# Softmax row sums from columns of ones beside the values, and routing logits gathered by transposes, in a fused attention and expert kernel

## The chip, the cores and the metric

The kernel runs on one core of a Trainium2 chip. The metric is the device time of one execution in microseconds; the median of the runs is compared. The engines are named as in the profile: PE is TensorE's matmuls and PEld its weight loads, DVE is VectorE, ACT is ScalarE, POOL is GpSimd, and SP is SyncE, which issues the loads here.

## The reference

Eight batches of eight heads, 576 positions in nine chunks of 64, 64 numbers to a head. Attention runs inside each chunk, and the result goes to an expert layer in which each of the 4,608 tokens takes one of eight experts.

```python
scores = scale * np.matmul(q_c, k_c.transpose(0, 1, 2, 4, 3))
scores = scores - np.max(scores, axis=-1, keepdims=True)
attn = np.exp(scores)
attn = attn / (np.sum(attn, axis=-1, keepdims=True) + 1e-09)
out = np.matmul(attn, v_c)
...
logits = x @ w_gate                      # x: 4608 x 512, w_gate: 512 x 8
expert_idx = np.argmax(logits, axis=1)
probs = softmax(logits); gate_w = probs[n, expert_idx[n]]
...
h = np.maximum(xe @ w1[e], 0.0)          # 512 -> 1024, for the tokens of expert e
out[mask] = gate_w[mask, None] * (h @ w2[e])
```

## The kernel before

**Two stages.** The attention stage computes the softmax attention, the logits and the routing; its end overlaps with the first slots of the expert stage, which gathers the tokens of an expert by indirect transfers (`xg`), multiplies them with weights that are split into a high and a low part (`whi`, `wlo`), and scatters the result. From about 110 us on the program is the expert stage.

**Groups.** The attention stage runs over 18 groups of two tiles. A tile is 128 rows (two chunks `c` of 64) with all eight heads; a head is `m` (2) times `hp` (4). The loop works on three groups at once. In iteration g, TensorE gets in this order: the scores of group g (64 products of 64x64, line 240, into the pair of banks S), the selection of the logits of group g-3 (`sel_`, line 1009), the transposes of the exponentials of g-1 into banks U and V (`attn_t`, line 288), the transposes of the attention result of g-2 into T and Q (`x_t`, line 322), the value products of g-1 back into U and V (`attn_v`, line 298), and the logits of g-2 into bank L (`logits_p`, line 334). Between `x_t` and `attn_v` every third group has four small matmuls of a routing step in bank K (lines 394 to 399).

**Softmax.** VectorE takes the row maximum `mx` (line 259), subtracts it (line 260), and sums the exponentials of the group before (`soft_c`, line 269). ScalarE computes the exponential (`soft_b`, line 265), adds 1e-9 to the sums (`soft_e`, line 275), and copies the transposes out of U and V (`at`, line 289) and out of T and Q (`xT`, line 324). VectorE then takes the reciprocal of the sums (`soft_d`, line 280) and multiplies: one product a tile, from bank U or V into the output block `xb` (`x_out`, line 312).

**Logits.** `logits_p` multiplies quarters of `xT` with the gate weights in four parts, 32 partitions apart, so that bank L gets 4 partial sums for each of eight experts, at partitions 0, 32, 64 and 96. ScalarE copies this to `lp` (line 1018). `sel_` multiplies `lp` with `sel_g`, a 0/1 matrix that adds the four parts and brings tokens onto partitions, eight columns a tile, into a place of bank L for a batch of 4 or 6 tiles. At a batch's end ScalarE copies the logits to `lg` (the step "c" of `route`, line 358), and `route` hands out its many small operations over the next groups.

**Order.** PE, DVE, ACT and POOL run in the program's order (a manual schedule). SyncE's queue is ordered by a planner, by when each load's buffer is ready. Its loads are 128x512 pieces of keys (`kb`, line 210) and queries (`qt`, line 212), halves of values (`vb`, line 216) and pieces of weights (`raw`, line 1031), 256 KB each. Eight are in flight; each load waits for the one eight places ahead of it. Three buffers `kb`, three `vb` and three `qt` are turned over; `load_qk(g+3)` and `load_v(g+2)` stand at the end of iteration g. A row of values of 64 positions has two groups of partitions, `m::2`, with zeros in the other's place: that is why `vb` is cleared at the start (by VectorE for `vb[0]`, by ScalarE for the other two).

Of the kernel before, what the change touches and what calls it, by code (L numbers as in the profile page):

```python
# [18 lines left out]
P = 128  # L19
NT = 4608  # L20
D = 512
# [25 lines left out]
def attn_moe_kernel(ctx: ExitStack, tc: tile.TileContext, q, k, v, wg, w, out):  # L47
# [76 lines left out]
    vb = [(ep if i == 1 else kv).tile([P, 2, G, 512], F32, name=f"vb{i}") for i in range(NB)]  # L124
# [14 lines left out]
    nc.vector.memset(vb[0], 0.0)  # L139
    for t in vb[1:]:  # L140
        nc.scalar.copy(t.rearrange("p m g x -> p (m g x)"), zero.broadcast_to([P, 2 * G * 512]))
    for _ in range(WARM):
        nc.tensor.matmul(pw, ones, ones.unsqueeze(1).broadcast_to([P, 4, P]), start=True, stop=True)
    for n in (192, 192, 192, BLK, BLK, BLK):
        nc.tensor.matmul(pw.rearrange("p a b -> p (a b)")[:, 0:n], warm[:, 0:P], warm[:, 0:n], start=True, stop=True)
    iota_i = xg[0][0][:, 0:P].bitcast(I32)
# [22 lines left out]
    nc.vector.tensor_scalar(ident, iota_f[:, 0:P], pid[:, 0:1], None, ALU.is_equal)  # L169
    tri = kv.tile([P, P], BF16, name="tri")  # L170
# [4 lines left out]
    sel_g = kv.tile([P, E], F32, name="sel_g")  # L175
    nc.vector.tensor_tensor(sel_g, ident[:, 0:E], ident[:, 32:32 + E], ALU.add)
    nc.vector.tensor_tensor(sel_g, sel_g, ident[:, 64:64 + E], ALU.add)
    nc.vector.tensor_tensor(sel_g, sel_g, ident[:, 96:96 + E], ALU.add)


# [46 lines left out]
    def keep(n):  # L227

        for _ in range(n):
            nc.tensor.matmul(pR.rearrange("p (a b) -> p a b", b=P), ones,  # L230
                             ones.unsqueeze(1).broadcast_to([P, 4, P]), start=True, stop=True)
# [45 lines left out]
    def soft_d(su):  # L277
        suf = su.rearrange("p h o -> p (h o)")
        ri = sm.tile([P, NH, 1], F32, name="ri", bufs=3)
        nc.vector.reciprocal(ri.rearrange("p h o -> p (h o)"), suf)  # L280
        return ri
# [9 lines left out]

    def attn_v(g, at):
        px = [one["U"], one["V"]]
# [7 lines left out]
        return px  # L301
# [3 lines left out]
    def x_out(g, px, ri, xt):  # L305
        r0 = g * G % RB

        t = g * G - XB * RB
        assert t < 0 or t in stored
        r4 = ri.rearrange("p (m i h) o -> p i h m o", i=G, m=2)  # L310
        for i in range(G):
            nc.vector.tensor_tensor(
                xt[:, r0 + i, 0:D].rearrange("p (m h d) -> p h m d", m=2, d=64),
                px[i].rearrange("p (h m d) -> p h m d", m=2, d=64),
                r4[:, i, :, :, :].broadcast_to([P, 4, 2, 64]), ALU.mult)
# [12 lines left out]
    pR = bank("K", [P, 512])  # L328
# [10 lines left out]
    def route(b, pl):  # L339
# [16 lines left out]
        yield "c"  # L356
        lg = small("lg")
        nc.scalar.copy(lg, pl[:, 0:n, :])
# [425 lines left out]
    def scratch(shape):  # L784
# [4 lines left out]
        t = vb[0].rearrange("p m g x -> p (m g x)")[:, used[0]:used[0] + n]  # L789
# [210 lines left out]
    pls = [None]  # L1000

    def sel_(g):
        b = [i for i in range(NBAT) if first[i] <= g * G][-1]
        if g * G == first[b]:
            o = b % 2 * NMAX * E
            pls[0] = pL[:, o:o + BATCHES[b] * E].rearrange("p (a b) -> p a b", b=E)
        lp = st_l.pop(g)
        for i in range(G):
            nc.tensor.matmul(pls[0][:, g * G - first[b] + i, :], lp[:, i * P:(i + 1) * P], sel_g,
                             start=True, stop=True)  # L1010
        if (g + 1) * G == first[b + 1]:
            r = route(b, pls[0])
            active.append([r, next(r), False])
# [32 lines left out]
    for g in range(NG):  # L1046
# [12 lines left out]
        if gl >= 1:  # L1059
            sel_(gl - 1)  # L1060
            advance("c")
        if ga >= 0:
# [3 lines left out]
            su = soft_c(st_e.pop(ga))  # L1066
        if gl >= 0:
            st_x[gl] = x_t(gl, xb[gl * G // RB % XB])
        if g + 1 < NG:
            if ga >= 0:  # L1070
                soft_e(su)
            st_e[g] = soft_a(ps, 1 if g else G)
            soft_b(st_e[g])
        else:
            soft_b(st_e[g])
            soft_e(su)
# [4 lines left out]
            turns["S"] = 0  # L1081
        pauses()
# [6 lines left out]
        if ga >= 0:  # L1089
            px = attn_v(ga, at)  # L1090
# [9 lines left out]
        if ga >= 0:  # L1100
            ri = soft_d(su)
            x_out(ga, px, ri, xb[ga * G // RB % XB])
# [12 lines left out]
    advance("c")  # L1115
    su = soft_c(ex)
# [3 lines left out]
    soft_e(su)  # L1120
    advance("a")
    st_x[g - 1] = x_t(g - 1, xb[(g - 1) * G // RB % XB])
    px = attn_v(g, at)
    advance("t")
    logits(g - 1)
    ri = soft_d(su)
    x_out(g, px, ri, xb[g * G // RB % XB])
# [4 lines left out]
    advance("c")  # L1132
# [12 lines left out]
    advance("c")  # L1145
# [181 lines left out]
```

## Time and profile before

| | before |
|---|---|
| median of 3 runs (lowest to highest) | 566.22 us (565.96 to 566.27) |
| the profiled execution, its span | 564.68 us, 562.9 us |
| PE busy | 550.6 us, 98% of the span |
| PEld busy | 489.4 us, 87% |
| DVE busy | 422.9 us, 75% |
| ACT busy | 278.4 us, 49% |
| POOL busy | 241.2 us, 43% |
| chain that ended last | PE 74%, issue 4%, POOL 1%, DVE 1% |
| granted TensorE clock, mean | 0.997 |

A busy share is an average over the whole program. The two stages have different limits, so the stretch of a stage says more than the table. The chain is followed back from the last instruction, at each step to what released it. In the timelines, rows of one operation that follow each other are put together: the first column is the start, the second the busy time of all of them, and xN is how many. An idle gap before a row stands in brackets, with what ended it. A busy matmul row overlaps the next one a little, so paces are read from starts.

### The profile page before, as it was taken

How to read it: one execution, taken by the hardware profiler on the slowest of the kernel's cores; microseconds unless marked ns; L12 is line 12 of the kernel's file. 1: busy time of each engine (PE TensorE's matmuls, PEld its weight loads, DVE VectorE, ACT ScalarE, POOL GpSimd, SP SyncE). 2: the span in 40 equal slices, each digit the busy share in tenths (PEclk: the TensorE clock that was granted, in tenths of full speed). 3: DMA queues.
4: the chain of work that ended last, by engine and by line, in shares of the span. 5: the costliest groups of instructions: out<-in, count | busy, mean ns of one | idle time of the engine just before them, and what ended most of it. 6: DMA issues, size and time to landing. Idle time of an engine off the chain costs nothing.

```text
span 562.9 us, 13225 instructions
## 1 busy us (share of the span) xinstructions
PE 550.6 (98%) x4735; PEld 489.4 (87%) x4735; DVE 422.9 (75%) x898; ACT 278.4 (49%) x473; POOL 241.2 (43%) x271
## 2 busy tenths in 40 slices
PE   7999999999999999999999999999999999999995
PEld 5788888788898989889998999988999998898993
DVE  7999999977677986988868875667666566766663
ACT  5667767651336553656546553444443444544332
POOL 3125665476533743537433642351515235250422
PEclk9999999999999999999999999999999999999998
DMA  8999999444764722265435633474522356211201
GB/s 299 381 368 358 398 388 398 153 170 160 267 220 142 237 83 54 68 205 171 146 127 151 211 87 114 157 281 132 215 61 81 120 164 210 65 36 29 68 2 58
DMA packets 51173, 99.03 MB, mean 176 GB/s; under 512 B 13696, under 2 KB 27008, under 8 KB 47488
## 3 DMA queue, kind: packets, MB, share of 16 engines
q0 software_dynamic: 18352, 58.30, 29.9%
q1 hardware_dynamic: 32432, 38.83, 20.4%
q8 instruction: 67, 1.10, 0.8%
q10 hardware_dynamic: 288, 0.52, 0.2%
q14 instruction: 34, 0.28, 0.2%
HBM read 106.59 MB, written 20.22 MB: 225 GB/s over the span
## 4 chain that ended last, share of the span: by engine, by line
PE 74%; issue 4%; POOL 1%; DVE 1%; ACT 0%; POOLq 0%; DVEq 0%
PE psS L637 26%; PE psL L637 8%; PE psU L735 5%; PE psU L736 5%; PE psU L737 5%; PE psV L735 5%; PE psV L736 5%; PE psV L737 5%; PE psK L750 2%; PE psK L748 2%; PE psS L641 2%; PE psK L736 1%; PE psK L737 1%; PE psK L735 1%; PE psT L620 1%
## 5 line engine op out<-in xcount | busy, mean ns | idle before, releaser
L77 DVE TENSOR_TENSOR wlo<-raw,whi 128x1024 fp32r<-128x1024 f32 x110 | 134.2, 1220 | 16.2 <-ACT whi L76 15.7
L686 ACT ACTIVATE h<-psS 128x384 fp32r<-128x384 f32 x84 | 41.3, 492 | 166.9 <-issue 122.1
L544 POOL DMA_INDIRECT raw<-in_w,widx x58 | 67.6, 1165 | 122.9 <-DVE wlo L77 57.5
L76 ACT CAST whi<-raw 128x1024 fp32r<-128x1024 f32 x110 | 114.7, 1043 | 0.0
L637 PE MATMUL psS<-xhi,whi 128*128 128x256 f32 (+2 forms) x368 | 113.9, 311 | 0.0
L637 PE MATMUL psS<-xhi,wlo 128*128 128x256 f32 (+2 forms) x368 | 113.1, 309 | 0.0
L637 PE MATMUL psS<-xlo,whi 128*128 128x256 f32 (+2 forms) x312 | 96.4, 309 | 0.0
L763 POOL DMA_INDIRECT out_y<-y,oid x40 | 44.1, 1102 | 105.6 <-ACTq L668 34.2
L645 DVE SCALAR_TENSOR_TENSOR hl<-psS,h 128x256 fp32r<-128x256 f32 x84 | 35.5, 423 | 57.7 <-ACT h L686 57.5
L562 POOL DMA_INDIRECT xg<-xd,idx x49 | 62.2, 1270 | 27.2 <-issue 13.6
L637 PEld LDWEIGHTS psS<-xhi,whi 128*128 128x128 f32 x368 | 69.3, 188 | 4.1 <-ACT xhi L626 0.5
L637 PEld LDWEIGHTS psS<-xhi,wlo 128*128 128x128 f32 x368 | 69.3, 188 | 0.6
L637 PEld LDWEIGHTS psS<-xlo,whi 128*128 128x128 f32 x312 | 58.6, 188 | 2.4
L735 PE MATMUL psU<-whi,h 128*128 128x512 f32 x120 | 48.3, 403 | 0.0
L735 PE MATMUL psV<-whi,h 128*128 128x512 f32 x120 | 47.3, 394 | 0.0
L736 PE MATMUL psU<-wlo,h 128*128 128x512 f32 x120 | 47.3, 394 | 0.0
L736 PE MATMUL psV<-wlo,h 128*128 128x512 f32 x120 | 47.1, 392 | 0.0
L737 PE MATMUL psU<-whi,hl 128*128 128x512 f32 x112 | 43.9, 392 | 0.0
L737 PE MATMUL psV<-whi,hl 128*128 128x512 f32 x112 | 43.9, 392 | 0.0
L441 POOL DMA_INDIRECT xd<-xb,di x32 | 31.7, 990 | 12.6 <-issue 6.9
L637 PE MATMUL psL<-xhi,wlo 128*128 128x320 f32 (+2 forms) x112 | 35.0, 313 | 0.2 <-issue 0.2
L637 PE MATMUL psL<-xlo,whi 128*128 128x320 f32 (+2 forms) x112 | 34.9, 312 | 0.0
(251 smaller groups left out, 1122.2 us busy)
## 6 DMA issues: line engine op xcount, KB each, us to landing
kb<-in_k SPq DMA_DIRECT2D x36, 256.0 KB
vb<-in_v SPq DMA_DIRECT2D x36, 256.0 KB
qt<-in_q SPq DMA_DIRECT2D x34, 256.0 KB
xg<-xg SPq DMA_DIRECT2D x208, 32.0 KB
raw<-in_w SPq DMA_DIRECT2D x16, 256.0 KB
raw<-in_w,widx POOLq DMA_INDIRECT x58, 4.5
xg<-xd,idx POOLq DMA_INDIRECT x49, 3.5
out_y<-y,oid POOLq DMA_INDIRECT x40, 3.2
```

What stands on the lines that cost most here:

```text
L76: nc.scalar.copy(hi, src)
L77: nc.vector.tensor_tensor(lo, src, hi.bitcast(F32), ALU.subtract)
L441: nc.gpsimd.indirect_dma_start(out=xds[t], out_offset=bass.IndirectOffsetOnAxis(ap=di[:, i, :], axis=0), in_=x, in_offset=None, bounds_che ...
L544: nc.gpsimd.indirect_dma_start(out=raw[c][:, :], out_offset=None, in_=w, in_offset=bass.IndirectOffsetOnAxis(ap=widx[:, u, c:c + 1], axis= ...
L562: nc.gpsimd.indirect_dma_start(out=t[:, :], out_offset=None, in_=xd[0:rows, :], in_offset=bass.IndirectOffsetOnAxis(ap=place(u, h), axis=0 ...
L637: nc.tensor.matmul(ph, a, b[:, kc, WIDE - ph.shape[1]:WIDE], start=kc + i == 0, stop=kc + i == 5 and not late)
L645: nc.vector.scalar_tensor_tensor(o, ph, 0.0, hi.bitcast(F32), ALU.max, ALU.subtract)
L686: nc.scalar.activation(hx[:, EXT:EXT + WIDE], ph, AF.Relu)
L735: nc.tensor.matmul(py, hh, wh, start=f == 0, stop=False)
L736: nc.tensor.matmul(py, hh, wl, start=False, stop=False)
L737: nc.tensor.matmul(py, hl, wh, start=False, stop=f == 7)
L763: nc.gpsimd.indirect_dma_start(out=outs[m], out_offset=bass.IndirectOffsetOnAxis(ap=oid[u % 3][:, m:m + 1], axis=0), in_=y, in_offset=None ...
```

## The change

**Row sums.** Each buffer of values is now eight blocks of 130 columns: a column of ones, 64 values of the first tile, 64 of the second, and a column of ones. The ones are written once (`side`, `sums_of`); they are laid out as the zeros are, ones for the partitions of the block's own half. A value product takes 65 columns of a block for each of two halves, the row sum being the outer column: 130 columns instead of 128. Three of a tile's four `hp` go to bank U or V, the fourth to the last 261 columns of bank K (`pK`); the routing's counts stay in the first 251 (`pR`). `soft_c` and `soft_e` are gone. `soft_d` comes directly behind `attn_v`: four ScalarE operations read the sums out of U, K, V and K, with 1e-9 added, and VectorE takes the reciprocal. `x_out` is three products: U, V and K.

**Values in memory.** The host lays values out so that a block of both tiles is together; a load writes columns 1 to 128 of each block, eight runs of 512 bytes a row in place of one of 4 KB. The rows of the gate weights and of the first expert matrix are permuted on the host to match the new order of heads.

**Logits.** `sel_` transposes `lp`, a tile at a time, into columns 0 to 127 and 384 to 511 of bank L; a reduction on VectorE (`sums`) adds the four parts a group, straight into `lg`. The step "c" is gone.

**Start.** Clearing `vb[1]` and `vb[2]` stands behind the warm-up matmuls in the text; clearing `vb[0]` stands behind the identity matrix, from which `side` is made.

```diff
-    vb = [(ep if i == 1 else kv).tile([P, 2, G, 512], F32, name=f"vb{i}") for i in range(NB)]
+    vb = [(ep if i == 1 else kv).tile([P, 2, 8, 130], F32, name=f"vb{i}") for i in range(NB)]
...
-    nc.vector.memset(vb[0], 0.0)
...
+    side = const.tile([P, 2, 1], F32, name="side")
+    nc.vector.tensor_reduce(side.rearrange("p m o -> p (m o)"), ident.rearrange("p (a m) -> p m a", m=2),
+                            AX.X, ALU.add)
+    nc.vector.memset(vb[0], 0.0)
+    def sums_of(t, put):
+        put(t[:, :, :, 0:130:129], side.unsqueeze(3).broadcast_to([P, 2, 8, 2]))
+    sums_of(vb[0], nc.vector.tensor_copy)
+    for t in vb[1:]:
+        sums_of(t, nc.scalar.copy)
...
     def load_v(g):
         for m in range(2):
-            nc.sync.dma_start(vb[g % NB][m::2, m, :, :], v[g, m::2, :, :])
+            nc.sync.dma_start(vb[g % NB][m::2, m, :, 1:129], v[g, m::2, :, :])
...
-    def soft_c(ex):
+    def soft_d():
         su = sm.tile([P, NH, 1], F32, name="su", bufs=2)
-        nc.vector.tensor_reduce(su.rearrange("p (m h) o -> p m (h o)", m=2),
-                                ex.rearrange("p h k m -> p m h k"), AX.X, ALU.add)
-        return su
-    def soft_e(su):
-        suf = su.rearrange("p h o -> p (h o)")
-        nc.scalar.activation(suf, suf, AF.Copy, bias=1e-9)
...
+        for i in range(G):
+            nc.scalar.activation(su[:, 6 * i:6 * i + 6, 0], one["UV"[i]][:, i * 64:i * 64 + 326:65], AF.Copy, bias=1e-9)
+            nc.scalar.activation(su[:, 12 + 2 * i:14 + 2 * i, 0], pK[:, i * 195:i * 195 + 66:65], AF.Copy, bias=1e-9)
+        nc.vector.reciprocal(ri.rearrange("p h o -> p (h o)"), su.rearrange("p h o -> p (h o)"))
...
+                to = one["UV"[i]][:, hp * 130:(hp + 1) * 130] if hp < 3 else pK[:, i * 131:i * 131 + 130]
                 for c in range(2):
-                    po, o = slice(c * 64, (c + 1) * 64), hp * 128 + c * 64
-                    nc.tensor.matmul(px[i][po, hp * 128:(hp + 1) * 128], at[:, i, hp, po],
-                                     vb[g % NB][:, :, i, o:o + 64],
+                    nc.tensor.matmul(to[po, :], at[:, i, hp, po], vb[g % NB][:, :, hp * 2 + c, i * 65:i * 65 + 65],
                                      start=True, stop=True, tile_position=(0, c * 64))
...
     def sel_(g):
         lp = st_l.pop(g)
         for i in range(G):
-            nc.tensor.matmul(pls[0][:, g * G - first[b] + i, :], lp[:, i * P:(i + 1) * P], sel_g,
-                             start=True, stop=True)
+            nc.tensor.transpose(p4[:, 3 * i, :], lp[:, i * P:(i + 1) * P], ident)
+    def sums(g):
...
+        nc.vector.tensor_reduce(lgs[0][:, o:o + G, :],
+                                p4.rearrange("p a (c e) -> p a e c", e=32)[:, 0::3, 0:E, :], AX.X, ALU.add)
```

**The load queue at the start.** SyncE, places 9 to 17 of the program's loads, before; `vb_122`, `vb_123` and `vb_124` are `vb[0]` to `vb[2]`, `kb_119` to `kb_121` are `kb[0]` to `kb[2]`. The waits name the DMA semaphore of the load eight places ahead and the engine that clears the buffer.

```order
L216 DMA vb_122<-in_v 64x1024 [waits DMAHW0_49,DVE_49]
L216 DMA vb_122<-in_v 64x1024 [waits DMAHW1_49]
L174 DMA wg_sb<-in_wg 128x4x8 [waits DMAHW2_49,Pool_49]
L210 DMA kb_121<-in_k 128x512 [waits DMAHW3_49]
L212 DMA qt<-in_q 128x512 [waits DMAHW4_49]
L210 DMA kb_121<-in_k 128x512 [waits DMAHW5_49]
L212 DMA qt<-in_q 128x512 [waits DMAHW6_49]
L216 DMA vb_123<-in_v 64x1024 [waits DMAHW7_49,Activation_49]
L216 DMA vb_123<-in_v 64x1024 [waits DMAHW0_49]
```

The same nine places of SyncE in the changed program:

```order
L214 DMA kb_121<-in_k 128x512 [waits DMAHW0_49]
L216 DMA qt<-in_q 128x512 [waits DMAHW1_49]
L214 DMA kb_121<-in_k 128x512 [waits DMAHW2_49]
L216 DMA qt<-in_q 128x512 [waits DMAHW3_49]
L184 DMA wg_sb<-in_wg 128x4x8 [waits DMAHW4_49,Pool_49]
L220 DMA vb_123<-in_v 64x8x128 [waits DMAHW5_49,Activation_49]
L220 DMA vb_123<-in_v 64x8x128 [waits DMAHW6_49]
L220 DMA vb_122<-in_v 64x8x128 [waits DMAHW7_49,DVE_49]
L220 DMA vb_122<-in_v 64x8x128 [waits DMAHW0_49]
```

The values of group 0 (`vb_122`) moved from the first two of these places to the last two; the keys and queries of group 2 and the values of group 1 moved ahead of them. The rest of this queue keeps its order.

**ScalarE in one group.** ScalarE in the middle of the stage, from the second copy of `x_t` to the cast of a weight piece, before:

```order
L324 COPY xT_643<-psQ 128x4x128 [waits PE_49]
L275 ACTIVATE su<-su 128x16 [waits DVE_49]
L265 ACTIVATE ex<-ex 128x1024 [waits DVE_49]
L1018 COPY lp<-psL 128x256 [waits PE_49]
L85 CAST whi_1_69<-raw_66 128x512 [waits DMAHW0_49]
```

The same piece of ScalarE in the changed program:

```order
L323 COPY xT_653<-psQ 128x4x128 [waits PE_49]
L269 ACTIVATE ex<-ex 128x1024 [waits DVE_49]
L275 ACTIVATE su<-psU 128x6 [waits PE_49]
L276 ACTIVATE su<-psK 128x2 [waits PE_49]
L275 ACTIVATE su<-psV 128x6
L276 ACTIVATE su<-psK 128x2
L1018 COPY lp<-psL 128x256 [waits DVE_49,PE_49]
L85 CAST whi_1_69<-raw_66 128x512 [waits DMAHW0_49]
```

The one operation on the sums stood ahead of the exponential; the four that read them stand behind it and wait for the value products. The copy of the logits also waits for VectorE now.

**VectorE in one group.** VectorE from the row sums of one group to its second product, before:

```order
L269 TENSOR_REDUCE su<-ex 128x16 [waits Activation_49]
L259 TENSOR_REDUCE mx<-psS 128x16 [waits PE_49]
L260 TENSOR_TENSOR ex<-psS,mx 128x2x512 [waits DVE_49]
L280 RECIPROCAL ri<-su 128x16 [waits Activation_49]
L312 TENSOR_TENSOR xb_116<-psU,ri 128x4x2x64 [waits DVE_49,PE_49]
L312 TENSOR_TENSOR xb_116<-psV,ri 128x4x2x64 [waits PE_49]
```

The same piece of VectorE in the changed program:

```order
L263 TENSOR_REDUCE mx<-psS 128x16 [waits PE_49]
L264 TENSOR_TENSOR ex<-psS,mx 128x2x512 [waits DVE_49]
L1009 TENSOR_REDUCE lg<-psL 128x16 [waits PE_49,Activation_49]
L277 RECIPROCAL ri<-su 128x16 [waits Activation_49]
L309 TENSOR_TENSOR xb_116<-psU,ri 128x384 [waits DVE_49,PE_49]
L309 TENSOR_TENSOR xb_116<-psV,ri 128x384 [waits PE_49]
L312 TENSOR_TENSOR xb_116<-psK,ri 128x2x128 [waits PE_49]
```

The row sums left the head of the group; the reduction of the logits came in behind the subtraction, and the two products became three.

## Rows read from the trace of the kernel before

**Rows 1.** Stretches: bounds, length, busy (count) by engine, granted clock, DMA share, GB/s.

```profile
20.00:45.00 25.00, 25.00 (x527) 21.66 (x523) 22.60 (x39) 18.12 (x38) 5.71 (x9) 1.00 1.01 364
```

**Rows 2.** Timeline of TensorE, one group: start, busy, line, operation, tiles, shapes, count.

```profile
27.57 1.16 PE L240 MATMUL psS<-kb,qt 64*64 64x64 f32 x64
28.66 0.61 PE L1009 MATMUL psL<-sel_g,lp 128*128 128x8 f32 x4
29.12 0.63 PE L288 MATMUL psU<-ident,ex 128*128 128x128 f32 x4
29.59 0.60 PE L288 MATMUL psV<-ident,ex 128*128 128x128 f32 x4
...
31.00 1.09 PE L298 MATMUL psU<-vb,at 128*64 128x128 f32 x16
...
32.90 0.64 PE L334 MATMUL psL<-xT,wg_sb 128*32 128x256 f32 x8
33.47 1.16 PE L240 MATMUL psS<-kb,qt 64*64 64x64 f32 x64
```

**Rows 3.** Timeline of VectorE, one group in the middle of the stage.

```profile
65.17 1.21 DVE L269 TENSOR_REDUCE su<-ex 128x16 f32<-128x1024 f32 x1
66.31 1.21 DVE L259 TENSOR_REDUCE mx<-psS 128x16 f32<-128x1024 f32 x1
67.55 1.23 DVE L260 TENSOR_TENSOR ex<-psS,mx 128x1024 f32<-128x1024 f32 x1
68.69 0.24 DVE L280 RECIPROCAL ri<-su 128x16 f32<-128x16 f32 x1
69.07 0.69 DVE L312 TENSOR_TENSOR xg<-psU,ri 128x512 f32<-128x512 f32 x1
```

**Rows 4.** Timeline of TensorE behind the loop, a selection and what follows it.

```profile
114.16 0.51 PE L1009 MATMUL psL<-sel_g,lp 128*128 128x8 f32 x4
114.52 1.19 PE L585 MATMUL psS<-ident,xg 128*128 128x128 f32 x8
```

**Rows 5.** Timeline of TensorE, the last two scores and the waits behind the last.

```profile
99.83 1.16 PE L240 MATMUL psS<-kb,qt 64*64 64x64 f32 x64
...
105.94 1.16 PE L240 MATMUL psS<-kb,qt 64*64 64x64 f32 x64
107.28 0.61 PE L1009 MATMUL psL<-sel_g,lp 128*128 128x8 f32 x4 [0.19 <-ACT lp L1018]
108.45 0.66 PE L288 MATMUL psU<-ident,ex 128*128 128x128 f32 x4 [0.55 <-DVE xb L312]
```

**Rows 6.** Timeline of ScalarE in the group of Rows 3.

```profile
65.12 0.18 ACT L422 ACTIVATE cb<-psK 128x8 f32<-128x8 f32 x1
65.19 0.19 ACT L423 ACTIVATE ce<-psK 128x8 f32<-128x8 f32 x1
...
68.81 1.06 ACT L265 ACTIVATE ex<-ex 128x1024 f32<-128x1024 f32 x1 [0.75 <-DVE ex L260]
69.77 0.35 ACT L1018 COPY lp<-psL 128x256 f32<-128x256 f32 x1
```

**Rows 7.** Timeline of SyncE's queue: start of issue, time of all, line, transfer, count.

```profile
15.57 0.42 SPq L212 DMA_DIRECT2D qt<-in_q  x1
...
93.62 6.86 SPq L216 DMA_DIRECT2D vb<-in_v  x4
```

**Rows 8.** Timeline of TensorE at the start: first value products, group 1's transposes.

```profile
12.90 1.09 PE L298 MATMUL psU<-vb,at 128*64 128x128 f32 x16 [0.24 <-ACT at L289]
...
17.27 0.66 PE L288 MATMUL psU<-ident,ex 128*128 128x128 f32 x4
```

**Rows 9.** DMA queues from 20 to 45 us: packets, MB, share of 16 engines.

```profile
q1 hardware_dynamic: 4335, 9.03, 99.6%
```

**Rows 10.** DMA packets and queues from 510 to 523 us.

```profile
DMA packets 1329, 0.73 MB, mean 56 GB/s; under 512 B 369, under 2 KB 1266, under 8 KB 1328
...
q1 hardware_dynamic: 1121, 0.46, 13.8%
```

More of the change, by code (lines that the diff above doesn't have):

```diff
@@ L169, in attn_moe_kernel @@
     nc.vector.tensor_scalar(ident, iota_f[:, 0:P], pid[:, 0:1], None, ALU.is_equal)
+    side = const.tile([P, 2, 1], F32, name="side")
[5 more added lines that the diff above has]
+    sums_of(vb[0], nc.vector.tensor_copy)
+    for t in vb[1:]:
+        sums_of(t, nc.scalar.copy)
     tri = kv.tile([P, P], BF16, name="tri")
@@ L229, in keep @@
         for _ in range(n):
-            nc.tensor.matmul(pR.rearrange("p (a b) -> p a b", b=P), ones,
+            nc.tensor.matmul(one["K"].rearrange("p (a b) -> p a b", b=P), ones,
                              ones.unsqueeze(1).broadcast_to([P, 4, P]), start=True, stop=True)
@@ L309, in x_out @@
         assert t < 0 or t in stored
[L310 removed]
+        o = xt[:, r0:r0 + G, 0:D].rearrange("p i (h d) -> p i h d", d=64)
         for i in range(G):
             nc.vector.tensor_tensor(
[L313 to L315 removed]
+                o[:, i, 0:6, :], one["UV"[i]][:, 1 - i:391 - i].rearrange("p (h d) -> p h d", d=65)[:, :, 0:64],
+                ri[:, 6 * i:6 * i + 6, :].broadcast_to([P, 6, 64]), ALU.mult)
+        nc.vector.tensor_tensor(
+            o[:, :, 6:8, :], pK[:, 1:261].rearrange("p (i h d) -> p i h d", i=G, d=65)[:, :, :, 0:64],
+            ri[:, 12:NH, :].rearrange("p (i h) o -> p i h o", i=G).broadcast_to([P, G, 2, 64]), ALU.mult)
     def x_t(g, xt):
@@ L327, in attn_moe_kernel @@
     pL = bank("L", [P, 512])
-    pR = bank("K", [P, 512])
+    pR = one["K"][:, 0:512 - 261]
     def logits_p(g, xT):
@@ L999, in attn_moe_kernel @@
     casts = []
-    pls = [None]
+    lgs = [None]
+    p4 = pL.rearrange("p (a t) -> p a t", t=P)
     def sel_(g):
+        lp = st_l.pop(g)
+        for i in range(G):
+            nc.tensor.transpose(p4[:, 3 * i, :], lp[:, i * P:(i + 1) * P], ident)
+    def sums(g):
         b = [i for i in range(NBAT) if first[i] <= g * G][-1]
         if g * G == first[b]:
[L1005 to L1008, printed above, removed]
-            nc.tensor.matmul(pls[0][:, g * G - first[b] + i, :], lp[:, i * P:(i + 1) * P], sel_g,
-                             start=True, stop=True)
+            lgs[0] = sm.tile([P, NMAX, E], F32, name="lg", bufs=2)[:, 0:BATCHES[b], :]
+        o = g * G - first[b]
+        nc.vector.tensor_reduce(lgs[0][:, o:o + G, :],
+                                p4.rearrange("p a (c e) -> p a e c", e=32)[:, 0::3, 0:E, :], AX.X, ALU.add)
         if (g + 1) * G == first[b + 1]:
-            r = route(b, pls[0])
+            r = route(b, lgs[0])
             active.append([r, next(r), False])
@@ L1081, in attn_moe_kernel @@
             turns["S"] = 0
+        if gl >= 1:
+            sums(gl - 1)
         pauses()
@@ L1089, in attn_moe_kernel @@
         if ga >= 0:
-            px = attn_v(ga, at)
+            attn_v(ga, at)
+            ri = soft_d()
         if g + 1 == NG:
@@ L1114, in attn_moe_kernel @@
     sel_(g - 2)
-    advance("c")
-    su = soft_c(ex)
+    sums(g - 2)
     pauses()
@@ L1131, in attn_moe_kernel @@
     sel_(g - 1)
-    advance("c")
+    sums(g - 1)
     advance("a")
@@ L1144, in attn_moe_kernel @@
     sel_(g)
-    advance("c")
+    sums(g)
     advance("a")
```

52 lines of the change are left out of this document (18 added, 34 removed).

## The prediction

> **What bounds the kernel now.** I read the stretches first, to see which resource is full in the attention stage; then TensorE's timeline of one group, for its pace; then the DMA queue's timeline; then VectorE and ScalarE in one group. The later stage I left alone: the edit has no line there, and the chain of waits is nearly all TensorE from there to the end, so I carry a shift of TensorE at 120 us to the end one for one.
>
> [rows 1] shows the attention stage with nearly everything full: TensorE 25.00 of 25 us, VectorE 22.60, the granted clock at 1.00 (the level of 2.4 GHz), and the 16 DMA engines at a share of 1.01. [rows 2] is one group of two tiles on TensorE: scores at 27.57, next scores at 33.47, so 5.90 us with no wait to speak of. VectorE needs less: in [rows 3] one group runs from 65.17 (row sums of the exponentials) over maximum, subtraction, reciprocal and the two products. Row sums to maximum is 1.14 us; the second product follows the first (69.07, 0.69 long) and ends near 70.3, a pace of 5.1 us. So TensorE sets the pace, VectorE follows at 86% of it, and the loads run some groups ahead of both. VectorE is what the edit relieves, and it isn't the bound.
>
> **The change part by part.**
>
> *TensorE, per group.* The two small matmuls against `sel_g` take 28.66 to 29.12, 0.46 us behind the scores [rows 2]; 0.36 in the tail, behind a full-size matmul [rows 4]. Two transposes take their place: four take 0.47 (29.12 to 29.59), so two 0.24, plus 0 to 0.10 for following the scores; I take 0.27. Gain 0.19 in a group, 0.14 in the tail. The value matmuls stream 130 columns for 128: 1.90 us (31.00 to 32.90) times 2/128 is 0.03 more. Net 0.16 less, 5.74 us a group. The new output starts at odd words of bank K; no row shows such a write, and I take no cost, with 0.9 us (half of 1.90) at most for one group as the far end.
>
> *VectorE.* The row sums go (1.14). The products cover the same 1,024 elements in three operations: 2 x 0.69 becomes about 1.45. A reduction of 64 logits comes, about 0.2. VectorE falls to some 4.3 us. That is worth nothing at a place where TensorE is the bound; it counts where TensorE waits for VectorE, at the end of the stage: [rows 5], 105.94 to 108.45 is 2.51 us for scores and selection, with idle gaps of 0.19 and 0.55 before the next transposes. Without waits these are 1.09 + 0.27 = 1.36: a gain of 1.15.
>
> *ScalarE and the new chain.* Four small reads of the sums stand where one small operation stood, but behind the exponential of the next group in ScalarE's queue, and the reciprocal and products wait for them. That makes a loop per group: maximum to subtraction 1.24, to exponential 1.26, to the next ScalarE operation 0.96 [rows 3, 6], three more at 0.07 apart and 0.18 for the last [rows 6], so 0.42 with the hand-over, reciprocal to product 0.38 [rows 3], products about 1.3. Sum 5.56 us, under TensorE's 5.74. The logits' reduction and up to five routing operations hide in VectorE's wait for ScalarE. Behind the waiting reciprocal stand the products, and for those the transposes into banks U and V; these are not needed before scores and selection have run, 1.9 us after the value matmuls end, and the first product ends about 1.4 us after. So this too I cost at nothing.
>
> *The start.* The queue of loads is built in another order: group 2's keys and queries and group 1's values now stand ahead of group 0's values, which were places 9 and 10 and become 16 and 17. Eight loads are in flight, each waiting for the one eight places ahead. The 17th load of before therefore had landed when the 25th was issued, 15.57 [rows 7]. The same nine loads stand at places 9 to 17 in both kernels, so group 0's value matmuls, which ran at 12.90, now wait until 15.6, and until 16.6 with the price of values below (four such loads). From there: value matmuls 1.9, sums, reciprocal and first product 1.4, transposes: 3.3 us later, where they stood at 17.27 [rows 8]. The shift of TensorE is 16.6 + 3.3 - 17.27 = 2.6 us, or 1.6 if values cost no more.
>
> *The loads of values.* Before, a row of 64 partitions got 4 KB in one run. Now each of its eight blocks is 512 bytes, between the columns of ones. The stage's loads move 9.03 MB in 25 us at 99.6% of 16 engines, 0.72 us for 256 KB; the only transfers in 512-byte runs, the 32 KB spreads, move 0.46 MB in 13 us at 13.8%, which is 1.02 us for 256 KB [rows 9, 10]. The difference, 0.30, is the upper end; the lower end is nothing, if the runs are streamed as before. Each 32 KB spread ends with its own completion packets, eight times as many per byte, and 369 of its 1,329 packets are these small ones, so I take 0.25. The Trainium skill (DMA: Bandwidth & Descriptors, Specifications) puts the line rate at 512 bytes and above; by it the loads would cost no more. The spreads' row speaks against that, and no run here shows it for loads from HBM.
>
> Does that reach TensorE? The lead of the loads is read at group 16. Its second half of keys had landed when the load eight places on was issued, 93.62, and its scores started at 99.83: a lead of 6.2 us [rows 5, 7]; the last query piece comes one place later and is needed half a scores stage later, the same 6.2. Fifteen groups of values, 30 loads, stand ahead: 30 x 0.25 = 7.5, so the data come 1.3 us late. TensorE alone would be at 2.6 - 13 x 0.16 = 0.5 late there. So the loads decide from about group 14 on, 1.3 us.
>
> *Sum.* At scores of group 16: +1.3. Group 17: -0.16, +1.1. Waits at the end of the stage: -1.15, so 0.0. Three selections in the tail at -0.14 and two sets of value matmuls: -0.35. Total -0.4 us, on a profiled execution of 564.68 us (span 562.9); the median of the runs is 1.54 above it, so 566.22 - 0.4 = 565.8. Each 0.01 us per load of values moves this by 0.3 while the loads decide: 0.30 gives +1.1. Below 0.22 TensorE decides again, and 0.20 gives -1.4 (start 2.4, thirteen groups -2.1, then -0.16, -1.15 and -0.35).
>
> **The rivals.**
>
> *Values cost no more.* For it: the bytes are the same and the source is one run. Against: [rows 10]. Then the start costs 1.6, fourteen groups give 2.2, the end 1.15, the tail 0.35: 564.1 us.
>
> *The new chain binds (slower).* If ScalarE's four reads don't overlap, each taking the 0.18 of its whole duration and a hand-over of some 0.07, they cost 1.0 in place of 0.42 and the loop is 6.14 us, 0.4 over TensorE's pace. It decides from 0.6 us for the four reads. Against the pace of before that is 0.24 a group, 3.4 in fourteen, on the start's 2.6, less the tail's 0.35, and the wait at the end stays: +5.6, 571.8 us. For it: the loop has 0.2 of room. Against: the two reads of bank K at 65.12 and 65.19 are 0.07 apart [rows 6].
>
> *Dearer loads (slower).* If a 512-byte run from HBM to a place that is one word off costs more than the spreads show, say 0.35 a load, the data are 4.3 late at group 16 and the sum is +2.6: 568.8 us. It decides from 0.31 a load. For it: no row has such a write. Against: it is one descriptor's work all the same.
>
> *The edit doesn't relieve what it is meant to* is no rival of its own: VectorE's relief is real but costs and gains nothing except at the stage's end, which is in the sum.
>
> **How the numbers follow.** Forecast 0.47, values at no cost 0.27, chain 0.10, dearer loads 0.12, anything else 0.04. What a measurement can tell from no change is about 0.2%, 1.13 us. The forecast's own range is 564.8 to 567.3 (0.20 to 0.30 a load), of which 0.08 is faster by more, 0.03 slower by more. Faster: 0.27 + 0.08 + 0.01 = 0.36. Slower: 0.10 + 0.12 + 0.03 + 0.03 = 0.28. Within: 0.36. The range reaches from 563.4, under the second case, to 569.0, over the dear loads; the chain lies outside, with some ends of the others.
>
> **What would show it.** In the changed profile: the first value matmuls near 16.6 us (15.6 if values are no dearer; 12.9 would refute the start); a group of 5.74 us between scores in the middle of the stage (5.90 or more refutes the gain); from group 14 on, scores that wait for loads, at 101.1 for group 16; the gap before the transposes behind the last scores gone; VectorE near 75% in the stage. In the timeline of ScalarE, four reads of the sums within 0.4 us, behind the exponential. I am wrong if the first value matmuls start early, if reads of the sums lie 0.2 apart, or if the DMA share falls below 1 before 90 us.

## The result, and the profile after

The changed kernel is slower: 573.58 us (573.13 to 574.84) against 566.09 us (564.29 to 566.27) for the kernel before on the same chip, a ratio of 1.0143 [1.0117, 1.0169], or 7.5 us. The profiled execution spans 571.7 us, 8.8 more than before. My forecast was 565.8 us, in a range of 563.4 to 569.0.

The loss is there when the attention stage ends. The timeline of TensorE after (start, busy, line, operation, count), from the last scores to the first product of the experts:

```profile
114.46 1.16 PE L244 MATMUL psS<-kb,qt 64*64 64x64 f32 x64
115.55 0.44 PE L1002 MATMUL psL<-ident,lp 128*128 128x128 f32 x2
116.59 0.66 PE L285 MATMUL psU<-ident,ex 128*128 128x128 f32 x4 [0.60 <-DVE xb L309]
...
126.84 0.39 PE L633 MATMUL psS<-xhi,whi 128*128 128x256 f32 x1
```

The last scores start 8.5 us later than in [rows 5] (105.94). From scores to transposes is 2.13 us where it was 2.51, so 0.4 comes back there. The first product of the experts, of which before's row follows, is 7.85 us late, and that shift stays between 7.3 and 8.3 us up to TensorE's last product.

```profile
118.99 0.39 PE L637 MATMUL psS<-xhi,whi 128*128 128x256 f32 x1
```

So the 8.5 us have to be found between the start and 114.46. The view of what TensorE waited for, after, from 17 to 107 us (total, times, longest), names two waits, neither of which is in before:

```profile
PE psU L297 <- DMA vb<-in_v: 4.6, 1, 4.6
PE psK L297 <- DVE dst L408: 4.3, 4, 1.5
```

**The start: +5.6.** TensorE after, from the first value products to the transposes of group 1:

```profile
17.36 1.57 PE L297 MATMUL psU<-vb,at 128*64 128x130 f32 x12 [4.63 <-DMA vb<-in_v]
...
21.03 1.94 PE L244 MATMUL psS<-kb,qt 64*64 64x64 f32 x64
22.90 0.66 PE L285 MATMUL psU<-ident,ex 128*128 128x128 f32 x4
```

The stretches after (length, busy and count by engine, granted clock, DMA share, GB/s) that go with it:

```profile
14.00:17.00 3.00, 0.00 (x0) 0.00 (x0) 0.26 (x1) 1.06 (x1) 0.00 (x0) 0.83 1.17 311
18.00:19.00 1.00, 1.00 (x14) 1.00 (x12) 0.00 (x0) 0.03 (x1) 0.00 (x0) 0.50 1.05 379
...
22.00:23.00 1.00, 1.00 (x41) 0.93 (x34) 1.00 (x3) 0.00 (x0) 0.97 (x1) 0.61 1.05 330
23.00:24.00 1.00, 1.00 (x10) 1.00 (x11) 1.00 (x2) 0.36 (x1) 0.30 (x1) 1.00 0.92 336
```

TensorE waits for the values and nothing runs on it from 14 to 17 us. The granted clock falls to 0.50, the level of 1.2 GHz, and is back at 1.00 at 23 us. The value products take 3.67 us (17.36 to 21.03) where they took 1.90, and the scores 1.87 (21.03 to 22.90) where they take 1.09. Transposes of group 1 stand at 22.90, 5.6 us behind [rows 8].

**Bank K: +5.0.** TensorE after, a group in which routing counts are in bank K:

```profile
47.92 0.89 PE L297 MATMUL psU<-vb,at 128*64 128x130 f32 x12
50.27 0.44 PE L297 MATMUL psK<-vb,at 128*64 128x130 f32 x4 [1.46 <-DVE dst L408]
```

VectorE over the same time:

```profile
48.24 1.23 DVE L264 TENSOR_TENSOR ex<-psS,mx 128x1024 f32<-128x1024 f32 x1
49.38 0.21 DVE L1009 TENSOR_REDUCE lg<-psL 128x16 f32<-128x64 f32 x1
...
50.05 0.17 DVE L408 TENSOR_TENSOR dst<-psK,oh_b 128x48 f32<-128x48 f32 x1
```

The fourth value product of a tile, the one that goes to bank K, waits until VectorE has read the counts of the routing out of that bank. From U's first product to K's is 0.72 us where nothing waits, and 2.35, 1.88, 1.79 and 1.87 in the four groups with this wait: 1.63 + 1.16 + 1.07 + 1.15 = 5.0 us.

**The rest.** Three rows of scores take longer, 1.32, 1.23 and 1.61 us for 1.16, and cost 0.8 together with small delays beside them; the longest has a short stop inside. The pace gains: one group without waits, after:

```profile
27.29 1.16 PE L244 MATMUL psS<-kb,qt 64*64 64x64 f32 x64
28.38 0.44 PE L1002 MATMUL psL<-ident,lp 128*128 128x128 f32 x2
28.66 0.60 PE L285 MATMUL psU<-ident,ex 128*128 128x128 f32 x4
...
32.99 1.16 PE L244 MATMUL psS<-kb,qt 64*64 64x64 f32 x64
```

That is 5.70 us for 5.90 in [rows 2]. From the scores at 27.29 to the last ones are fourteen groups, and they give 2.9; 0.4 of it are small delays of the kernel before in its last two groups (6.39 and 6.11 us from scores to scores, for 6.22 and 5.90 elsewhere). The sum is 5.6 + 5.0 + 0.8 - 2.9 = 8.5 us, the shift at the last scores.

VectorE is relieved as meant, 17.81 us of 25 where [rows 1] has 22.60. The loads are not, in this stretch and in the queue of SyncE's loads:

```profile
20.00:45.00 25.00, 25.00 (x537) 21.38 (x538) 17.81 (x34) 17.40 (x48) 5.22 (x5) 0.94 1.03 337
```

```profile
q1 hardware_dynamic: 7652, 8.34, 101.4%
```

At a full share they move 8.34 MB where [rows 9] has 9.03, in 7,652 packets for 4,335.

### The profile page after: what moved, and what is told of

The parts are those of the page before. It is cut to its first block, busy times and chain, and to the rows that moved or that the text cites. A ratio compares the mean times of both kernels' runs of the same rounds, so it can differ in the third digit from the quotient of the medians.

```text
span 571.7 us, 13252 instructions
## 1 busy us (share of the span) xinstructions
PE 550.7 (96%) x4699; PEld 488.6 (85%) x4699; DVE 410.4 (72%) x915; ACT 282.4 (49%) x521; POOL 236.9 (41%) x271
## 4 chain that ended last, share of the span: by engine, by line
PE 72%; issue 4%; POOL 1%; DVE 1%; ACT 0%; POOLq 0%; DVEq 0%
PE psS L633 25%; PE psL L633 8%; PE psU L733 5%; PE psU L731 4%; PE psU L732 4%; PE psV L733 4%; PE psV L732 4%; PE psV L731 4%; PE psK L744 2%; PE psK L746 2%; PE psS L637 1%; PE psK L731 1%; PE psK L732 1%; PE psK L733 1%; PE psT L616 1%
## 5 line engine op out<-in xcount | busy, mean ns | idle before, releaser
L540 POOL DMA_INDIRECT raw<-in_w,widx x58 | 65.6, 1131 | 125.3 <-DVE wlo L77 56.4
L87 POOL TENSOR_TENSOR wlo<-raw,whi 128x512 fp32r<-128x512 f32 x16 | 20.5, 1288 | 35.1 <-ACT whi L85 35.0
```

The costliest lines, as they stand in the source:

```text
L540: nc.gpsimd.indirect_dma_start(out=raw[c][:, :], out_offset=None, in_=w, in_offset=bass.IndirectOffsetOnAxis(ap=widx[:, u, c:c + 1], axis= ...
```

## The experiments

My theory after the result was the ledger above: three separate costs (start, bank K, values in runs of 512 bytes), and a gain of 0.2 us a group under them. The rivals: each cost hides another, so that removing one gives nothing; the transposed logits are the cost; the runs of 512 bytes cost nothing. The chips of the runs differ: on some the kernel before takes 566 us, on others 575, with the same last scores and the loss behind them (106.28 and then rows like the one below), so every ratio is against the kernel before on the same chip, and positions are compared up to the last scores.

```profile
119.78 0.38 PE L298 MATMUL psV<-vb,at 128*64 128x128 f32 x2 [1.01 <-issue]
```

That row is TensorE's in c_before, the kernel before unchanged, which ran once (573.76 us). c_after, the changed kernel unchanged, took 583.71 us on such a chip, 1.0188 [1.0092, 1.0285], with the last scores at 114.54. Where such rows of single products fall ahead of the last scores, as in a_keep and a_pad_wait, the position of the last scores tells little.

> The kernel before, for its trace on a chip of these runs. Both theories: the stage as in the first trace (last scores near 105.9 us); what this chip takes more lies behind it, or the stage itself is later and the stage's times of the other kernels have to be compared with this trace.

> The changed kernel again, as the mark for the other three on this chip. Both theories: 7 to 9 us over the kernel before (573 to 575 us where that takes 566), TensorE's first value products at about 17.4 us, four waits of 0.9 to 1.5 us on line 297.

### Bank K: value products ahead of the routing in the text

```diff
         advance("t")
+        if ga >= 0:
+            attn_v(ga, at)
         if g + 1 < NG:
             small_op(5)
         if ga >= 0:
-            attn_v(ga, at)
             ri = soft_d()
```

TensorE and VectorE get the same instructions in the same order. What turns round is the wait: in the changed kernel `L297 MATMUL psK<-vb,at` waits for a VectorE semaphore in the groups with counts, and here it doesn't.

> The changed kernel with one move in its text: the routing's small VectorE operations of a group (the reading of the counts in bank K among them) stand behind the value products in place of ahead of them. No engine gets another order of instructions; the wait turns round: the count's reader waits for the value products' writes to bank K, not these for the reader. Theory (a write to one part of bank K is held until VectorE has read the counts in another part of it): the four waits of TensorE on line 297 (4.3 us of idle, 5.0 us counted from start to start) are gone, 573.6 - 5.0 = 568.6 us. Rival (VectorE's own order makes the group late, and the wait only moves to the next transposes): 572.5 to 573.6 us, with gaps of about 1 us at line 285 or 244 in the same four groups.

TensorE in a_small, the group shown above:

```profile
46.66 0.89 PE L297 MATMUL psU<-vb,at 128*64 128x130 f32 x12
47.37 0.39 PE L297 MATMUL psK<-vb,at 128*64 128x130 f32 x4
```

The product into K follows at once, 1.4 us ahead of VectorE's read (at 48.78). All four waits are gone, and the last scores stand at 110.45, 4.1 us earlier than in c_after. Of these, 1.3 us stand already at the scores of group 3 (26.02 for 27.34), ahead of the first of the waits, since in this execution the values came earlier (16.80) and the clock was low for a shorter time. So 2.8 of the 5.0 us are kept, and the rest goes to other delays: one wait of 1.3 us for a copy of ScalarE, and short stops. The time is 582.47 us, 1.0126 [1.0071, 1.0181] on a chip of the 575 kind. The trace shows the wait and what causes it; in time, an interval of 6 us on such a chip doesn't tell 4 us from 1.

### The start: place of the loads, and the clock

In a_start2 `vb[0]` is cleared early, and its ones are written at the end of iteration 0, which gives the queue of loads the order of before:

```diff
     nc.gpsimd.memset(zero, 0.0)
+    nc.vector.memset(vb[0], 0.0)
...
-    nc.vector.memset(vb[0], 0.0)
...
-    sums_of(vb[0], nc.vector.tensor_copy)
...
         side_op(4)
+        if g == 0:
+            sums_of(vb[0], nc.vector.tensor_copy)
```

> The changed kernel with the first buffer of values cleared early, as before, and its ones written at the end of the first group, so that the loads stand in the order of the kernel before (group 0's values at places 9 and 10). Theory (the start costs 3.1 us of waiting for data and 2.5 us at the lower clock): value products at about 13, the granted clock at 1.00 throughout, 573.6 - 5.6 = 568.0 us. Rival (the loads of values set the end of the stage, so an earlier start is lost again there): 570.5 us or more, with scores of groups 14 to 17 waiting for loads.

TensorE in a_start2:

```profile
12.51 0.89 PE L296 MATMUL psU<-vb,at 128*64 128x130 f32 x12 [0.24 <-ACT at L285]
...
17.02 0.69 PE L243 MATMUL psS<-kb,qt 64*64 64x64 f32 x32 [1.89 <-issue]
...
20.90 0.89 PE L296 MATMUL psU<-vb,at 128*64 128x130 f32 x12 [1.29 <-ACT at L285]
```

The value products are back at 12.51 at full clock, so the place in the queue is what moved them. But the second half of the next scores waits to 17.02, and the value products of group 1 wait for ScalarE, which stands at a cast of weights behind a load:

```profile
19.74 0.62 ACT L85 CAST whi<-raw 128x512 fp32r<-128x512 f32 x1 [4.58 <-DMA raw<-in_w]
```

Of the 4.85 us at the first products 3.9 are left at the scores of group 3 (23.39 for 27.29), and 0.6 at the last scores (113.86 for 114.46). So at the last scores the start by itself gains almost nothing, as the rival of hidden costs had it. What takes the gain back in between is 0.9 us in one row of scores with a stop, 1.8 in a group with a stop and a wait of 1.25 for ScalarE, and 0.4 more at bank K; the scores of groups 14 to 17 don't wait for loads, which the expectation's rival had named. The time is 581.92 us, 1.0096 [1.0065, 1.0127], an interval that overlaps c_after's.

a_keep takes away the clock's part alone. TensorE runs 18 matmuls of its warm-up while it waits for the values:

```diff
+        if ga == 0:
+            keep(18)
         if ga >= 0:
             attn_v(ga, at)
```

> The changed kernel with 18 matmuls of ones into bank K put ahead of the first value products, so that TensorE works while it waits for the first values. Theory (the wait itself brings the clock down): granted clock 1.00 from 14 to 24 us, value products of group 0 in 1.9 us in place of 3.7, 573.6 - 2.5 = 571.1 us. Rival (the clock falls for another reason, or lost time at the start is hidden by late loads): 573.6 us.

TensorE and one stretch in a_keep:

```profile
12.58 4.05 PE L234 MATMUL psK<-ones 128*128 128x512 bf16 x18
17.19 0.89 PE L297 MATMUL psU<-vb,at 128*64 128x130 f32 x12 [0.56 <-issue]
...
19.11 1.16 PE L244 MATMUL psS<-kb,qt 64*64 64x64 f32 x64
```

```profile
17.00:20.00 3.00, 2.81 (x91) 2.67 (x95) 0.33 (x2) 0.95 (x5) 0.00 (x0) 1.00 1.05 346
```

The values come at the same time, the clock stays at 1.00, and the value products take 1.92 us. Two scores later TensorE is 2.3 us ahead of the changed kernel (25.01 for 27.29), 0.2 of it by an earlier start of the products: 2.1 us are the clock's part of the start. It isn't kept: in this execution waits at K (5.4 us), for ScalarE's copies (2.3) and on issue (2.4) come later, for a reason that this run doesn't show, the last scores stand at 119.1, and 582.92 us is 1.0122 [1.0062, 1.0183].

a_both2 (first chip) and c_both2 (a second one) have the edits of a_small and a_start2 together.

> Both moves at once. Theory (two independent losses): 573.6 - 5.0 - 5.6 = 563.0, plus up to 1.5 for loads that now come late at the end of the stage (0.16 to 0.2 us more for each load of values): 563.0 to 564.5 us, the first version of the new scheme below the kernel before. Rival (each load of values costs 0.25 us more, as the forecast had it): loads decide from group 14 on and the time is 565.8 us. Rival (the chain over ScalarE sets the pace once the waits are gone): groups of 5.9 us or more, 567 us or more.

> Both moves again (the values of group 0 loaded in their old places, the small routing operations behind the value products), beside the unmoved changed kernel on one chip. Theory (the start and the waits at bank K are the whole loss): 8 to 10 us under the changed kernel, 563 to 566 us where the kernel before takes 566. Rival (the loads of values, 0.25 us dearer each, take over): 5 to 8 us under the changed kernel, 566 to 568, with scores or copies that wait for loads from the first groups on. Rival (the chain over ScalarE): groups of 5.9 us without a wait for loads.

a_both2 took 579.32 us, 1.0046 [1.0010, 1.0082], and c_both2 580.83, 1.0076 [1.0036, 1.0116], with the last scores at 109.5 and 110.5. c_both2 is under c_after on the same chip by some 6 us by the ratios and 3 by the medians, where two independent losses would have given 8 to 10. Start and bank K are then repaired, and the kernel is still slower than before. So something else costs, and of the change the layout of the values, the logits and the new chain are left.

### The parts alone, in the kernel before

b_logits puts the transposes and the reduction of the logits into the kernel before, whose VectorE still has the row sums:

```diff
-            nc.tensor.matmul(pls[0][:, g * G - first[b] + i, :], lp[:, i * P:(i + 1) * P], sel_g,
-                             start=True, stop=True)
+            nc.tensor.transpose(p4[:, 3 * i, :], lp[:, i * P:(i + 1) * P], ident)
...
+        if gl >= 1:
+            sums(gl - 1)
```

> The kernel before with one part of the change alone: the logits' quarters transposed (two full transposes a group in place of the two products with the 0/1 matrix, a reduction of 64 numbers on VectorE, no copy at a batch's end). Row sums, value loads and the start stay as before. Theory (TensorE's time per group counts): 15 groups at -0.19 and the tail: 3.0 us under the kernel before, 563.1 where that takes 566.1. Rival (VectorE, busy 22.6 of 25 us, takes the 0.2 us and the stage ends no sooner): 0 to 1 us under, with the gap before the last transposes grown by 2 us.

574.86 us, 1.0000 [0.9967, 1.0033]: not the cost, and by itself no gain. A group without waits takes 5.67 us for 5.90, but VectorE is busy for 23.94 us of 25 in the stretch below, where the kernel before has 23.92 and no such wait, and TensorE now waits for it, 2.4 us in five places, here 0.59 us for the reduction:

```profile
70.00:95.00 25.00, 24.00 (x527) 20.48 (x526) 23.94 (x53) 17.30 (x37) 14.89 (x22) 1.00 1.04 392
```

```profile
88.16 0.64 PE L328 MATMUL psL<-xT,wg_sb 128*32 128x256 f32 x8 [0.59 <-DVE lg L1004]
```

b_runs gives the kernel before the blocks of 130 columns, without ones in use, and loads in runs of 512 bytes:

```diff
-            nc.sync.dma_start(vb[g % NB][m::2, m, :, :], v[g, m::2, :, :])
+            nc.sync.dma_start(vb[g % NB][m::2, m, :, 1:129], v[g, m::2, :, :])
```

> The kernel before with one part of the change alone: the values in blocks of 130 columns, loaded in runs of 512 bytes in place of 4 KB, the outer columns unused; row sums, logits and start as before. Theory (0.25 us more a load): the share of the DMA engines stays full, loads are 1.3 us late at group 16, 567.4 us where the kernel before takes 566.1 (1 to 2.5 us over it). Rival (0.16, as the steps between landings say): the lead of 6.2 us holds, no change. Rival (the price of the shares, 0.30, and more at the start, where nothing is ahead): 3 us or more over it, with waits from the first groups on.

578.09 us, 1.0060 [1.0027, 1.0094], or 3.4 us (1.6 to 5.4). Its queue of loads from 20 to 45 us:

```profile
q1 hardware_dynamic: 7782, 8.57, 102.9%
```

At a full share again less than before's 9.03 MB. The last four loads of values, SyncE's queue in c_before and in b_runs:

```profile
94.14 6.68 SPq L216 DMA_DIRECT2D vb<-in_v  x4
```

```profile
99.06 6.00 SPq L216 DMA_DIRECT2D vb<-in_v  x4
```

They are issued 4.9 us later, when the load eight places ahead has landed; 30 loads of values stand ahead of that one, so 0.16 us each. That is an estimate, since TensorE's own lateness holds buffers too. From the megabytes and shares of the changed kernel I get 0.24. The dear runs are the third cost in time, the size of the rival with waits from the first groups on. They act at once: TensorE waits 1.43 us for ScalarE (0.49 in c_before) before the value products of group 1, because a cast stands behind a load, and the scores of group 3 are 1.1 us late. The last scores are 3.9 us late; the other 2.8 stand in three groups with a short stop in their scores, and keys lie 5.2 us ahead at group 16 (104.24 - 99.06). Whether the runs are dear for their length or for starting one column off, and whether they bring on the stops, no run shows.

### All three removed

In a_pad the host lays the ones out beside the values, so that a row is again one run, of 4,160 bytes; the ones are no longer written in the kernel, `vb[0]` is cleared early, and the value products stand ahead of the routing as in a_small.

```diff
-            nc.sync.dma_start(vb[g % NB][m::2, m, :, 1:129], v[g, m::2, :, :])
+            nc.sync.dma_start(vb[g % NB][m::2, m, :, :], v[g, m::2, :, :])
...
-    vh = np.ascontiguousarray(vh.reshape(NG, P, 8, 128))
+    vh = np.pad(vh.reshape(NG, P, 8, 128), ((0, 0), (0, 0), (0, 0), (1, 1)), constant_values=1)
```

a_pad_wait is the same with the routing ahead of the value products, as in the changed kernel.

> The changed kernel with the ones brought along by the loads: the host lays each row of values out in blocks of 130 with a one at either side, so that a load writes one run of 4,160 bytes a row in place of eight of 512, no instruction writes ones, and the first buffer can be cleared and loaded as early as before; the routing's small operations stand behind the value products. Theory (runs of 512 bytes, the place of the first values in the load queue and the turn of the wait at bank K are the whole loss; what is left is TensorE's gain): last scores at 103.1 us (105.94 before), groups of 5.7 us, loads 3 us ahead, 3 to 3.5 us under the kernel before (ratio 0.994). Rival (the chain over ScalarE, or VectorE with the logits' reduction, sets the pace once nothing else does): groups of 5.8 to 6.1 us, no gain or some loss against the kernel before.

> The same with the small routing operations in their place in the changed kernel, ahead of the value products, so that only the wait at bank K is back. Theory: four waits of TensorE, 5.0 us counted by starts, last scores at 108.1, 4.5 to 5 us over the kernel with both moves. Rival (they lie beside other waits): under 2 us over it.

On a chip of the 575 kind: a_pad 0.9999 [0.9969, 1.0029], a_pad_wait 1.0021 [0.9987, 1.0055]. a_pad's last scores stand at 108.1, 5 us later than expected, and it gains nothing there. The four waits are back in a_pad_wait, 4.9 us in its view of waits, but the two times can't be told apart: the difference is 1.3 us, and by the two intervals at most about 4. So the 4.5 to 5 us expected for the waits did not come on this chip, and the rival of under 2 us fits. On a chip of the 566 kind I ran a_pad again as a_pad_2, with three copies in which a piece of TensorE's program starts elsewhere, since the scores had short stops that no load or engine explained:

```diff
-            nc.tensor.addr_align(64, offset=48, max_nops=0)
+            nc.tensor.addr_align(64, offset=0, max_nops=0)
```

> The version with padded values and both moves again, as the mark for the three next to it. Theory (short stops of TensorE in the middle of scores, without a late load, eat its gain): the same stops again in about the same groups, last scores at 107 to 109 us, the time within 0.3% of the kernel before. Rival (they were chance of one execution): last scores near 103 to 104 us and 3 us under the kernel before.

> The same with one number changed: TensorE's program from group 3 on starts 16 places earlier within a stretch of 64 (offset 0 in place of 48, which is 16 further on). Theory (the stops come where the next block of TensorE's program is fetched, and that transfer waits among the loads): the stops move to other matmuls of the group, and the time changes by 1 us or more either way. Rival (something in the scores themselves): the stops stay in the scores, time unchanged.

> The same with offset 16. Theory: as for offset 0, the stops at another place of the group. Rival: unchanged.

> The same with offset 32. Theory: as for offset 0, the stops at another place of the group. Rival: unchanged.

a_pad_2 took 564.30 us against 566.02, 0.9965 [0.9948, 0.9982]. It beats both kernels, by 1.7 us over before and some 9 to 10 us, 1.6 to 1.8%, over the changed one. So the three costs together are all of the loss, and under them is a small gain. How the loss divides among them is read from traces; in time, only the runs of 512 bytes are shown by themselves (b_runs). a_pad_2 also leaves out the writing of the ones, which no run tests by itself. The places 0, 16 and 32 gave 0.9969 [0.9953, 0.9986], 0.9977 [0.9955, 1.0000] and 0.9988 [0.9967, 1.0009], each interval reaching over the others, while the short stops moved to other groups: the place of the program is not shown to matter in time. TensorE in a_pad_2, one such stop, and the end of the stage:

```profile
75.85 0.82 PE L234 MATMUL psS<-kb,qt 64*64 64x64 f32 x39 [0.55 <-issue]
...
105.38 1.16 PE L234 MATMUL psS<-kb,qt 64*64 64x64 f32 x64
106.47 0.44 PE L992 MATMUL psL<-ident,lp 128*128 128x128 f32 x2
106.75 0.60 PE L275 MATMUL psU<-ident,ex 128*128 128x128 f32 x4
```

The keys lie some 5 us ahead there. What ends such stops can be read from the DMA records: queue q8 brings 16 KB of instructions at a time, about one transfer for 240 instructions of TensorE, and one ran from 73.35 to 74.27. In a_pad_2 from 73 to 74 us:

```profile
q8 instruction: 1, 0.02, 5.8%
```

In all seventeen traces together, 38 stops of 0.2 us or more lie inside rows of scores between 20 and 106 us, and each ends 1.3 to 1.6 us after a transfer of this queue. The transfers come some 6 us apart, so this is no chance: by it TensorE waits there for its own program, though no run changes these transfers alone. Why they come late in some groups and not in others (the kernel before has no such stop) stays open; in a_pad_2 the groups with them are 1.8 us longer than others, about what its gain falls short of the 3 to 3.5 expected of a_pad.

## Why the prediction was wrong, point by point

- **TensorE per group: right.** 5.70 us for a forecast of 5.74. The odd words of bank K cost nothing that shows: from the first product's start, four into K take 0.22 us (31.22 to 31.44), where twelve into U take 0.72.
- **VectorE: right.** 17.81 of 25 us, and not the bound. In b_logits, with the row sums still on VectorE, TensorE waits for it; that the second part of the change pays only with the first is argued, not shown.
- **ScalarE's loop, a rival: did not come.** The four reads run 0.05 to 0.07 apart, as forecast. ScalarE after, in one group:

```profile
42.96 1.09 ACT L269 ACTIVATE ex<-ex 128x1024 f32<-128x1024 f32 x1
43.91 0.20 ACT L275 ACTIVATE su<-psU 128x6 f32<-128x6 f32 x1
43.97 0.21 ACT L276 ACTIVATE su<-psK 128x2 f32<-128x2 f32 x1
44.02 0.23 ACT L275 ACTIVATE su<-psV 128x6 f32<-128x6 f32 x1
44.08 0.24 ACT L276 ACTIVATE su<-psK 128x2 f32<-128x2 f32 x1
```

- **The start: mechanism right, term too small, +3.0.** The forecast was a shift of 2.6 us, it was 5.6. The values came at 17.36, not 16.6 (0.8). The step that failed is "3.3 us later": it took durations from a TensorE at 1.00 and put them behind a wait of 4.6 us. With the clock at 0.50 it was 5.54 (17.36 to 22.90). In a_keep, at 1.00, the same stretch is 3.44 (17.19 to 20.63), so 2.1 us are the clock.
- **Bank K: missed, +5.0.** "This too I cost at nothing" followed who waits behind the reciprocal on VectorE, and not who waits for VectorE on bank K. The columns of counts and sums don't overlap, yet the program makes the product wait for the read. The wait stands in the changed program's order, on TensorE's first product into K in each group with counts; the pieces of order that the prediction rests on are ScalarE's and VectorE's, not TensorE's. In the ledger this term, or the start's 3.0, would by itself turn the forecast gain of 0.4 into a loss; in time no run shows it alone.
- **The loads of values: size near, place wrong.** 0.16 to 0.24 us a load, by two estimates, for a forecast of 0.25, and the rival without a cost falls with b_runs. But "the loads decide from about group 14 on" did not come: scores of group 16 stand at 108.76, not 101.1, without waiting, since TensorE is itself so late that keys lie 5.3 us ahead (108.76 less 103.44, the issue of the load eight places on). In b_runs too no late scores wait for keys. What can be traced of the dear runs there is 1.1 us through a cast of ScalarE at the start, a path that the prediction didn't have. The price of 0.25 rests in part on a misread row: the 1,329 packets of [rows 10] are those of all queues, and the queue of the spreads has 1,121 of them. With start and K repaired (a_both2, c_both2) the kernel stays 0.5 to 0.8% over before, which is the size of b_runs' 0.6%.
- **End of the stage: right only without disturbance.** 2.13 us after, for a forecast of 1.36; a routing operation of VectorE took 1.42 us there. In a_pad_2 it is 106.75 - 105.38 = 1.37.
- **The sum.** The forecast had +1.1 at the last scores, set by the loads; TensorE alone would have been at +0.3 (2.6 less fourteen groups of 0.16). Measured: 8.5. To the 0.3 come 3.0 at the start, 5.0 at K and 0.8 of slower scores, less 0.6 of more pace (2.9 for 2.3), of which 0.4 are before's own delays. The terms add up in this one trace; repaired one at a time they don't (a_small kept 2.8 of 5.0, a_start2 0.6 of 5.6 at the last scores).

## What to carry to other kernels

Ask of every bank or buffer that a change gives a second user who reads or writes it last in the text, whatever columns each uses, and look for that wait on the bounding engine in the order of the changed program; here turning two lines of text round took the wait away. Price what runs behind a new long wait of TensorE at its lower clock. If a DMA queue is full, keep runs in one piece and let the host lay out the constants: here runs of 512 bytes cost some 3 us (b_runs), and runs of 4,160 bytes with the ones in them nothing that shows (a_pad_2). Repair all suspected costs at once as well as one by one: here no single repair showed clearly in the time, and all three together did.

## What the runs showed of the hardware

- Loads from HBM in runs of 512 bytes, written one column off into rows of 130, took some 0.16 to 0.24 us more per 256 KB than runs of 4 KB at a full share of the DMA engines (8.34 MB in the changed kernel and 8.57 in b_runs, for 9.03 in 25 us); these are estimates from such figures.
- In the wait of 4.63 us the granted clock fell to 0.50 (0.83 on the mean from 14 to 17 us, 0.50 from 17 on), and it came back between 22 and 23 us (0.61 on the mean), with TensorE at work since 17.36. With matmuls in the gap (a_keep) it stayed at 1.00. Shorter waits went either way: after one of 2.43 us in a_pad_2 the clock was 0.50 from 11 to 13 us and the scores took 1.94 us, after one of 2.41 us at the same place in c_after it was 1.00 and they took 1.16.
- Short stops inside rows of scores, 0.2 to 1.4 us from one product's start to the next's, ended 1.3 to 1.6 us after a 16 KB transfer of the instruction queue q8, 38 times in 38.
- Chips ran the same program 9 us apart (566 and 575 us). In the traces of the kernel before on two of them the last scores lie 0.3 us apart, the first product of the experts 5.5 (118.99 and 124.45) and the end 9.1: the difference lies behind the last scores, where TensorE gets its products one or two at a time.
